# Pooled attention and a GELU MLP: key pools of batches 3 to 7 turned by a transposing DMA, with pools kept at 72 rows per head

## Chip, cores and metric

The kernel runs on one core of a Trainium2 chip. The metric is the device time of one launch in microseconds (us); lower is better. Names used below: PE is TensorE's matmul stream, PEld its weight loads, DVE is VectorE, ACT is ScalarE, POOL is GpSimd, SP is SyncE, which in this kernel only issues DMAs.

## What is computed

Attention over pooled keys and values, then a two-layer MLP with a tanh GELU, in float32 at the borders:

```python
# q, k, v: (8 batches, 8 heads, 576 rows, 64); pool = 8, so Sp = 72 pools per head
k_p = k.reshape(B, H, Sp, 8, D).mean(axis=3);  v_p = v.reshape(B, H, Sp, 8, D).mean(axis=3)
scores = (1 / sqrt(D)) * q @ k_p.T ;  attn = exp(scores - max);  attn /= attn.sum(-1) + 1e-9
x = (attn @ v_p).transpose(0, 2, 1, 3).reshape(4608, 512)
h = x @ w_in                                   # 512 -> 2048
g = 0.5 * h * (1 + tanh(sqrt(2/pi) * (h + 0.044715 * h**3)))
out = g @ w_out                                # 2048 -> 512, 4608 rows
```

## The kernel before, in words

**Stages.** The order of instructions is written out by hand: every engine runs its instructions in the order in which the program issues them, and a DMA instruction that has to wait holds back everything behind it on the engine that issues it. After a prologue (batch 0's attention) there are nine groups, g = 0 to 8, each of 512 rows of x (a batch has 576). A group has two phases on PE. P1 (`p1_mm`, line 332; `gelu`, line 338) is 64 matmuls of 512 columns, x times `w_in`, with one GELU on ACT for each of 16 blocks `fo`. P2 (`p2_mm`, line 343; `store`, line 349) is 64 matmuls of 512 columns, g times `w_out`, in four row tiles r of 16 matmuls, each copied out of PSUM by DVE into a tile `osb` and stored by four DMAs on SP. The attention of the next batch, nb = g + 1, is spread over P2: at the positions `pos = (6, 14, 20, ...)` of line 506, counted in P2 matmuls, `qk` makes the scores of one pair of heads for half a batch, `expo` takes exp on ACT, and one position later `av` multiplies with the pooled v (which also holds columns of 8.0, so that the sums come out beside the products); `norm` and `mult` divide. So the first `qk` of a batch stands before P2 matmul 6, the first `av` before P2 matmul 14. Groups 7 and 8 have no attention. The last row tile of group 8 is done in two column parts of 384 and 128 columns (line 532).

**What feeds the attention of batch b.** Three loads, issued by POOL in `load_next` (line 449) at the start of group b - 2 (for batch 2 after P1 of group 0; batches 0 and 1 are loaded from the prologue):

- q (`load_q`, line 83), cast to bf16 on the way into `qb`; `trans_q_dma` (line 221) turns it into `qT` by a transposing DMA that SP issues once the load has landed. POOL then waits for `qT` at the copy into `gate` (line 453) before it issues the other loads.
- k (`load_k`, line 67) as 512 + 64 rows of pools, whatever head they belong to: 128 partitions x 4 rows, and the remaining 64 rows in a fifth column of `kt`, beside 64 rows of v.
- v (`load_v`, line 78), pools 0 to 63 of each head.

In group b - 1, DVE adds up the eight rows of each pool: `k_steps` (line 140; 1280, 640 and 320 elements per partition) at fo 2 and 3, giving `kp`, and `v_steps` (line 154) at fo 7 and 8, giving the main part of `vp`. The last 8 pools of v, which lie in `kp`, are moved into rows of `vp` by two small DMAs that SP issues (`v_moves`, line 148). PE turns `kp` at fo 9 by five transposes (`trans_k_mm`, line 169), and DVE copies the result into the two weight tiles `kTs` (`trans_k_copy`, line 175, 12 copies a batch, most of them small). Because the v rows of heads 4 to 7 are kept in a rotated order on 128 partitions, `kTs`, `vp` and `ones` have 128 columns or rows for these heads (`pool_rows`, line 231).

**Order on the two queues around the change.** On SP, in each group: the `qT` transposing DMA of batch g + 2, the two `v_moves` of batch g + 1, then the 16 stores of the group. On POOL, in each group: the load of q, the copy into `gate`, the loads of k and v. Batch 1 differs: its q is transposed on PE in group 0 (fo 12 to 15), and its v is loaded by SP from the prologue (line 422), held back by a one-element memset of `vt` on DVE (line 421).

Of the kernel before, what the change touches and what calls it, by code (L numbers as in the profile page):

```python
# [18 lines left out]
def kernel(  # L19
# [23 lines left out]
    KR = 4  # L43
# [9 lines left out]
    opool = ctx.enter_context(tc.tile_pool(name="op", bufs=6))  # L53
# [11 lines left out]
    kts = [consts.tile([128, KR + 1, 512], F32, name=f"kt{i}") for i in range(2)]  # L65

    def load_k(b, engs):
        rows = k[b].rearrange("h (j l) d -> (h j) (l d)", l=8)
        main = rows[0:128 * KR].rearrange("(p r) c -> p r c", r=KR)
        n = KR // len(engs)  # L70
        for i, eng in enumerate(engs):
            eng.dma_start(out=kts[b % 2][:, i * n:(i + 1) * n], in_=main[:, i * n:(i + 1) * n])
        engs[0].dma_start(out=kts[b % 2][64:128, KR], in_=rows[128 * KR:])
        rows = v[b].rearrange("h (j l) d -> j h (l d)", l=8)
        for i in range(2):
            engs[-1].dma_start(out=kts[b % 2][32 * i:32 * i + 32, KR], in_=rows[64:, 4 * i:4 * i + 4])  # L76
# [41 lines left out]
    kTs = [[consts.tile([128, H, 128], BF16, name=f"kT{i}{e}") for e in range(2)] for i in range(2)]  # L118
    kps = [consts.tile([128, KR + 2, D], BF16, name=f"kp{i}") for i in range(2)]

    vps = [consts.tile([128, H, 2, D], BF16, name=f"vp{i}") for i in range(2)]

    vz = consts.tile([128, H, 2, D], BF16, name="vz")
    ones = consts.tile([128, 2, 3, D], BF16, name="ones")
# [6 lines left out]
    for half, j0, j1 in ((0, 0, 128), (1, 0, 8), (1, 64, 128)):  # L131
        nc.vector.memset(ones[j0:j1, half, 1], 8.0)
# [14 lines left out]

    def v_moves(b):

        for i in range(2):  # L150
            nc.sync.dma_start(out=vps[b % 2][64 - 64 * i:72 - 64 * i, 4 * i:4 * i + 4, 0],
                              in_=kps[b % 2][32 * i:32 * i + 32, KR])

    def v_steps(b):
        t = vts[b % 2]
        w = (vps[b % 2] if b else vz)[:, :, 0]

        def main():
            for i in range(2):
                p = slice(64 * i, 64 * i + 64)  # L160
                add(w[p, 4 * i:4 * i + 4], t[p, :, 0:64], t[p, :, 64:128])

        return [lambda: add(t[:, :, 0:256], t[:, :, 0:256], t[:, :, 256:512]),
                lambda: add(t[:, :, 0:128], t[:, :, 0:128], t[:, :, 128:256]), main]
# [10 lines left out]
    def trans_k_copy(b, e, bank, lower=True, upper=True):  # L175


        tp = half_bank(bank)[0:D, 0:(KR + 1) * 128].rearrange("p (r c) -> p r c", c=128)
        o = kTs[b % 2][e][e * 64:(e + 1) * 64]
        copy = nc.vector.tensor_copy  # L180

        def heads(h0, h1, c0, j0, j1):
            copy(out=o[:, h0:h1, c0:c0 + (j1 - j0) * KR].rearrange("p h (j r) -> p h j r", r=KR),  # L183
                 in_=tp[:, 0:KR, h0 * KH:h1 * KH].rearrange("p r (h j) -> p h j r", j=KH)[:, :, j0:j1])

        if lower:
            heads(0, 4, 0, 0, KH)
        if upper:
            heads(4, H - 1, 64, 0, 16)
            heads(4, H - 1, 0, 16, KH)  # L190
            copy(out=o[:, H - 1, 64:72].rearrange("p (j r) -> p j r", r=KR),
                 in_=tp[:, 0:KR, (H - 1) * KH:128].rearrange("p r j -> p j r"))
            copy(out=o[:, H - 1, 72:128], in_=tp[:, KR, 64:120])
            copy(out=o[:, H - 1, 0:8], in_=tp[:, KR, 120:128])
# [36 lines left out]
    def pool_rows(pr):  # L231
        return Sp if pr < PR // 2 else 128

    def qk(b, c, pr, bank):
        for e in range(2):
            h = 2 * pr + e
            n = pool_rows(pr)
            nc.tensor.matmul(out=PS[:n, bank + e, :CH].rearrange("j (t p) -> j t p", p=32),  # L238
                             lhsT=kTs[b % 2][c][:, h, :n],
                             rhs=qTs[b][:, h // 4, :, h % 4 * 32:h % 4 * 32 + 32],  # L240
                             start=True, stop=True)

    def expo(b, c, pr, bank):
        n = pool_rows(pr)
        e = ep.tile([128, 2, CH], BF16, name="e", bufs=8)
        nc.scalar.activation(out=e[:n], in_=PS[:n, bank:bank + 2, :CH], func=ACT.Exp, scale=1.0 / 64.0)  # L246
        es[b, c, pr] = e
# [6 lines left out]
    def av(b, c, pr, bank):  # L254


        e = es.pop((b, c, pr))
        n = pool_rows(pr)
        for x in range(2):
            nc.tensor.matmul(out=PS[:, bank + x, :CH], lhsT=window(vps[b % 2][:n], 2 * pr + x),  # L260
                             rhs=e[:n, x, :], start=True, stop=True)
# [20 lines left out]
    def den0(c, pr, bank):  # L282
        for x in range(2):
            e = es[0, c, pr + x]
            n = pool_rows(pr)
            for y in range(2):
                one = ones[:n, pr // 2].rearrange("j a d -> j (a d)")[:, 64 - 64 * y:192 - 64 * y]
                nc.tensor.matmul(out=PS[:, bank + x, :CH], lhsT=one, rhs=e[:n, y, :],
                                 start=(y == 0), stop=(y == 1))
# [8 lines left out]
    def av0(c, pr, bank):  # L298
        for x in range(2):
            e = es.pop((0, c, pr + x))  # L300
            n = pool_rows(pr)
            for y in range(2):
                nc.tensor.matmul(out=PS[:, bank + x, :CH], lhsT=window(vz[:n], 2 * (pr + x) + y),
                                 rhs=e[:n, y, :], start=(y == 0), stop=(y == 1))
# [27 lines left out]
    def p1_mm(g, fo, ko, c0=0, c1=GROUP):  # L332
        r0 = g * GROUP
        q, j = divmod(fo % 8, 4)
        nc.tensor.matmul(out=PS[:, h_bank(g, fo), c0:c1], lhsT=w_in_b[fo // 8][:, ko, q * 512 + j:(q + 1) * 512:4],  # L335
                         rhs=xT[:, ko, r0 + c0:r0 + c1], start=(ko == 0), stop=(ko == KO - 1))
# [10 lines left out]
    osbs = {}  # L347

    def store(g, r, bank, c0=0, c1=DM):
        if (g, r) not in osbs:  # L350
            osbs[g, r] = opool.tile([128, DM], F32, name="osb")
        osb = osbs[g, r]
        nc.vector.tensor_copy(out=osb[:, c0:c1], in_=PS[:, bank, c0:c1])  # L353

        for n in range(4):
            b, col = divmod(g * GROUP + r * 128 + n * 32, S)
            rows = out[b * S:(b + 1) * S].rearrange("(p t e) d -> e t p d", t=TP, e=2)
            eng = nc.scalar if c1 - c0 < DM and n % 2 else nc.sync
            eng.dma_start(out=rows[col // CH, col % CH // 32, :, c0:c1], in_=osb[n * 32:(n + 1) * 32, c0:c1])
# [30 lines left out]
    for h in range(H):  # L390
        i = h // 4
        nc.tensor.matmul(out=PS[64 - 64 * i:72 - 64 * i, 7, h * D:(h + 1) * D],
                         lhsT=identb[0:64, 32 * i + h % 4:32 * i + 32:4], rhs=kps[0][0:64, KR],
                         start=True, stop=True)
# [3 lines left out]
    for i in range(2):  # L398
        p = slice(64 - 64 * i, 72 - 64 * i)
        nc.vector.tensor_copy(out=vz[p, 4 * i:4 * i + 4, 0],  # L400
                              in_=PS[p, 7, 256 * i:256 * i + 256].rearrange("p (h d) -> p h d", d=D))
# [18 lines left out]

    nc.vector.memset(vts[1][:, 0, 0:1], 0.0)
    load_v(1, [nc.sync])
# [13 lines left out]
    for w in vps:  # L436
        nc.vector.memset(w, 8.0)
        nc.vector.memset(w[0:64, H // 2:], 0.0)
        nc.vector.memset(w[0:8, H // 2:], 8.0)
# [5 lines left out]
    for g in range(NG):  # L445
# [3 lines left out]
        def load_next():  # L449

            load_q(g + 2)
            trans_q_dma(g + 2)
            nc.gpsimd.tensor_copy(out=gate, in_=qTs[g + 2][0:1, 1, TP - 1, 0:2])  # L453
            load_k(g + 2, [nc.gpsimd])
            load_v(g + 2, [nc.gpsimd])

        if 0 < g and g + 2 < B:
            load_next()
# [3 lines left out]
        if nb is not None:  # L462
            kk = k_steps(nb)
# [3 lines left out]
            if g:  # L467
                plan = {2: kk[:1], 3: kk[1:], 7: vv[:1], 8: vv[1:], 9: tk}
            else:
                tq = [lambda a=a, i=i: trans_q(nb, *a, (5, 6, 7, 5)[i], nc.vector) for i, a in enumerate(QG)]  # L470
                plan = {0: kk, 12: tq[:1], 13: tq[1:2] + tk, 14: tq[2:3], 15: tq[3:] + vv}
# [13 lines left out]
        for fo, ko in first:  # L485
            p1_mm(g, fo, ko)
        for fo in range(FO):
            if fo >= 4:
                for ko in range(KO):
                    p1_mm(g, fo, ko)  # L490
# [41 lines left out]
    for c0, c1, bank in ((0, 384, o_bank(g, 3)), (384, DM, 4)):  # L532
        for fo in range(FO):
            p2_mm(g, 3, fo, bank, c0, c1)
        store(g, 3, bank, c0, c1)
# [30 lines left out]
```

The softmax here doesn't subtract the row's maximum and nothing guards it: scores larger than these inputs give would overflow.

## Time and profile before

| | before |
|---|---|
| median of 3 runs | 307.33 us (307.14 to 310.01) |
| the profiled execution: its own time | 307.9 us |
| its span in the profile | 306.1 us |
| PE busy | 296.8 us (97%) |
| PEld busy | 157.6 us (51%) |
| DVE busy | 150.5 us (49%) |
| ACT busy | 219.0 us (72%) |
| POOL busy | 35.0 us (11%) |
| P1 to P2 to next P1, group 3 (first matmuls) | 119.29, 133.39, 151.13 us |
| 128x512 matmuls, lines 335 and 344 | 126.6 and 133.9 us busy |

The span runs from the first to the last instruction of the trace; the execution's own time is 1.8 us longer. "Busy" of PE counts the modelled length of matmuls that overlap, so distances between starts say more than lengths: two consecutive matmuls of 512 columns start 0.216 us apart. A line of the timeline gives the start, the length, the engine, the source line, the operation and its tiles, and how many instructions it sums up; the brackets give the idle time before them and who ended it. A DMA stands in the timeline with the time that its issue took on the issuing engine (SPq, ACTq, POOL), not with its transfer. In lists of groups the columns are line, engine, operation, tiles, shapes, count, busy us, mean ns, and idle time before.

### The profile page before, as it was taken

How to read it: one execution, taken by the hardware profiler on the slowest of the kernel's cores; microseconds unless marked ns; L12 is line 12 of the kernel's file. 1: busy time of each engine (PE TensorE's matmuls, PEld its weight loads, DVE VectorE, ACT ScalarE, POOL GpSimd, SP SyncE). 2: the span in 40 equal slices, each digit the busy share in tenths (PEclk: the TensorE clock that was granted, in tenths of full speed). 3: DMA queues.
4: the chain of work that ended last, by engine and by line, in shares of the span. 5: the costliest groups of instructions: out<-in, count | busy, mean ns of one | idle time of the engine just before them, and what ended most of it. 6: DMA issues, size and time to landing. Idle time of an engine off the chain costs nothing.

```text
span 306.1 us, 4354 instructions
## 1 busy us (share of the span) xinstructions
PE 296.8 (97%) x1528; PEld 157.6 (51%) x1557; DVE 150.5 (49%) x336; ACT 219.0 (72%) x402; POOL 35.0 (11%) x67
## 2 busy tenths in 40 slices
PE   8999899999999999999999999999999999999994
PEld 3555455555555555555555555555555555445543
DVE  5885757572577057805682559245932630120012
ACT  1687489867987798779977898789868986206500
POOL 7102002305003200320014000400000000000000
PEclk9999999999999999999999999999999999999999
DMA  7999987977955962696159827672101210121022
GB/s 221 266 254 264 227 171 139 310 168 184 257 138 113 278 154 53 118 279 154 35 112 250 181 61 103 203 153 71 35 1 36 59 44 0 36 70 35 2 68 69
DMA packets 30806, 41.12 MB, mean 134 GB/s; under 512 B 18176, under 2 KB 18432, under 8 KB 29888
## 3 DMA queue, kind: packets, MB, share of 16 engines
q0 software_dynamic: 7568, 24.38, 33.7%
q1 hardware_dynamic: 22528, 15.14, 21.1%
q10 hardware_dynamic: 688, 1.31, 1.3%
q8 instruction: 12, 0.20, 0.3%
q14 instruction: 10, 0.08, 0.1%
HBM read 36.70 MB, written 9.44 MB: 151 GB/s over the span
## 4 chain that ended last, share of the span: by engine, by line
PE 87%; DMA 11%; issue 1%; ACT 0%; DVE 0%; POOLq 0%
PE PS L344 40%; PE PS L335 37%; DMA qb<-in_q_dram 11%; PE PS L238 5%; PE PS L260 4%; PE PS L173 1%; PE PS L203 0%; ACT e L246 0%; ACT ld L268 0%; ACT ld L267 0%; DVE osb L353 0%; POOLq L550 0%
## 5 line engine op out<-in xcount | busy, mean ns | idle before, releaser
L344 PE MATMUL PS<-w_out_b,gT 128*128 128x512 bf16 (+2 forms) x577 | 133.9, 373 | 0.7
L335 PE MATMUL PS<-xT,w_in_b 128*128 128x512 bf16 x563 | 126.6, 379 | 0.7
L341 ACT ACTIVATE gT<-PS 128x512 bf16<-128x512 f32 x144 | 81.2, 603 | 48.1 <-PE PS L335 48.0
L335 PEld LDWEIGHTS <-w_in_b 128*128 128x128 bf16 x576 | 64.7, 113 | 57.2
L344 PEld LDWEIGHTS <-gT 128*128 128x128 bf16 x592 | 57.0, 97 | 55.7 <-issue 0.4
L353 DVE COPY osb<-PS 128x512 f32<-128x512 f32 (+2 forms) x37 | 25.1, 677 | 98.2 <-PE PS L344 78.6
L278 DVE TENSOR_TENSOR xT<-PS,rc 64x288 bf16<-64x288 f32 x112 | 50.9, 455 | 31.7 <-ACT rc L270 27.5
L246 ACT ACTIVATE e<-PS 72x576 bf16<-72x576 f32 (+1 forms) x64 | 41.0, 647 | 8.8 <-PE PS L238 7.9
L238 PE MATMUL PS<-qT,kT 128*72 128x288 bf16 (+1 forms) x128 | 25.8, 286 | 0.9 <-ACT qT L213 0.6
L270 ACT ACTIVATE rc<-ld 128x288 f32<-128x288 f32 x56 | 24.8, 444 | 1.8
L313 ACT ACT_TABLE_LOAD x17 | 21.8, 1283 | 4.3 <-issue 4.1
L267 ACT ACTIVATE ld<-PS 64x288 f32<-64x288 f32 x56 | 22.8, 408 | 1.3
L268 ACT ACTIVATE ld<-PS 64x288 f32<-64x288 f32 x56 | 22.5, 402 | 1.4
L260 PE MATMUL PS<-e,vp 72*128 72x288 bf16 (+1 forms) x112 | 23.1, 286 | 0.0
L138 DVE TENSOR_TENSOR kt<-kt 128x1280 f32<-128x1280 f32 (+5 forms) x18 | 18.9, 1048 | 7.6 <-DMA kt<-in_v_dram 4.6
L238 PEld LDWEIGHTS <-kT 128*72 128x72 bf16 (+1 forms) x128 | 13.2, 105 | 15.1 <-DVE qT L215 1.2
L453 POOL COPY gate<-qT 1x2 bf16<-1x2 bf16 x6 | 1.0, 174 | 138.5 <-DMA qT<-qb 138.5
L138 DVE TENSOR_TENSOR vt<-vt 128x1024 f32<-128x1024 f32 (+1 forms) x16 | 15.3, 956 | 1.7 <-DMA vt<-in_v_dram 1.4
L183 DVE COPY kT<-PS 64x288 bf16<-64x288 bf16 (+2 forms) x48 | 13.0, 318 | 6.2 <-PE PS L173 6.0
L260 PEld LDWEIGHTS <-vp 72*128 72x128 bf16 (+1 forms) x112 | 11.0, 98 | 3.8
L365 PE MATMUL PS<-idle 128*128 128x512 bf16 x32 | 10.4, 468 | 1.6 <-DVE idle L126 1.2
L76 POOL DMA_DIRECT2D kt<-in_v_dram x14 | 8.0, 586 | 0.1
(48 smaller groups left out, 88.8 us busy)
## 6 DMA issues: line engine op xcount, KB each, us to landing
out_dram<-osb SPq DMA_DIRECT2D x140, 64.0 KB
kt<-in_k_dram POOLq DMA_DIRECT2D x7, 1024.0 KB, 6.0
vt<-in_v_dram POOLq DMA_DIRECT2D x12, 512.0 KB, 8.7
qb<-in_q_dram POOLq DMA_DIRECT2D x7, 576.0 KB, 11.8
w_in_b<-in_moe_w_in_dram POOLq DMA_DIRECT2D x2, 1024.0 KB, 16.8
w_out_b<-in_moe_w_out_dram POOLq DMA_DIRECT2D x4, 512.0 KB, 19.3
vt<-in_v_dram SPq DMA_DIRECT2D x3, 512.0 KB
kt<-in_k_dram POOLq DMA_DIRECT2D x7, 128.0 KB, 6.0
```

The costliest lines, as they stand in the source:

```text
L138: nc.vector.tensor_tensor(out=o, in0=a, in1=b, op=ALU.add)
L238: nc.tensor.matmul(out=PS[:n, bank + e, :CH].rearrange("j (t p) -> j t p", p=32), lhsT=kTs[b % 2][c][:, h, :n], rhs=qTs[b][:, h // 4, :, h ...
L246: nc.scalar.activation(out=e[:n], in_=PS[:n, bank:bank + 2, :CH], func=ACT.Exp, scale=1.0 / 64.0)
L260: nc.tensor.matmul(out=PS[:, bank + x, :CH], lhsT=window(vps[b % 2][:n], 2 * pr + x), rhs=e[:n, x, :], start=True, stop=True)
L267: nc.scalar.activation(out=ld[0:64], in_=PS[64:128, bank, :CH], func=ACT.Ln)
L268: nc.scalar.activation(out=ld[64:128], in_=PS[0:64, bank + 1, :CH], func=ACT.Ln)
L270: nc.scalar.activation(out=rc, in_=ld, func=ACT.Exp, scale=-1.0)
L278: nc.vector.tensor_tensor(out=xT[rows, pr, col:col + CH], in0=PS[rows, bank + x, :CH], in1=rc[rows], op=ALU.mult)
L335: nc.tensor.matmul(out=PS[:, h_bank(g, fo), c0:c1], lhsT=w_in_b[fo // 8][:, ko, q * 512 + j:(q + 1) * 512:4], rhs=xT[:, ko, r0 + c0:r0 + c ...
L341: nc.scalar.activation(out=gTs[g][:, fo, :], in_=PS[:, h_bank(g, fo), :], func=ACT.Gelu_apprx_tanh)
L344: nc.tensor.matmul(out=PS[:, bank, c0:c1], lhsT=gTs[g][:, fo, r * 128:(r + 1) * 128], rhs=w_out_b[:, fo, c0:c1], start=(fo == 0), stop=(fo ...
L353: nc.vector.tensor_copy(out=osb[:, c0:c1], in_=PS[:, bank, c0:c1])
```

## The change

Four things change.

1. **Keys of batches 3 to 7** (`KX = 3`). k is loaded with 72 pools of each head on 72 partitions, 8 heads side by side (`load_k_dma`). DVE adds it there (2048, 1024 and 512 elements per partition), writes the pools into a zeroed tile `kz` and copies them to a second place in it (`k_steps_dma`, now at fo 0); SP issues a transposing DMA from `kz` into `kx`, whose blocks are the weights of `qk`. PE's five transposes and DVE's copies of these batches go. The last 8 pools of v go to partitions 96 to 127 of `kt`, are added by three more small instructions, and moved into `vp` by two DMAs as before.
2. **Order.** For nb of 3 and later, `load_next` is issued after the transposing DMA of `kz`, not at the start of the group, and begins with a copy into `gate` that reads `kx`. On SP the order of such a group is: `kx` of batch g + 1, `qT` of batch g + 2, the two `v_moves` of batch g + 1, the 16 stores. In group 6 there is no load any more.
3. **v and the pool rows.** v keeps its 72 rows in order; `kTs`, `vp`, `vz` and `ones` shrink to 72 rows or columns; the k copies of batches 0 to 2 are 8 a batch, `v_moves` of batches 1 and 2 one DMA. v of batch 1 is loaded (by SP) after the first add of batch 1's k in group 0. `osb` has 5 buffers instead of 6. POOL zeroes `kz` once.
4. **The last group.** P1 of group 8 is done in 384 + 128 columns for every fo, the last 128 read from `xT` with a step of 32 elements, so that the last row tile's rows come out in another order; its P2 is done in 256 + 256 columns, each half stored by one DMA (the first by ACT, the second by SP) instead of four.

```diff
+    kts = [consts.tile([128, H, 512], F32, name=f"kt{i}") for i in range(2)]
+    KX = 3
...
-        for i in range(2):
-            engs[-1].dma_start(out=kts[b % 2][32 * i:32 * i + 32, KR], in_=rows[64:, 4 * i:4 * i + 4])
+        engs[-1].dma_start(out=kts[b % 2][0:64, KR], in_=rows[64:])
+
+    def load_k_dma(b):
+        nc.gpsimd.dma_start(out=kts[b % 2][0:Sp], in_=k[b].rearrange("h (j l) d -> j h (l d)", l=8))
+        rows = v[b].rearrange("h (j l) d -> j h (l d)", l=8)
+        for y in range(2):
+            nc.gpsimd.dma_start(out=kts[b % 2][96:128, y], in_=rows[64 + 4 * y:68 + 4 * y])
...
+    def k_steps_dma(b):
+        t = kts[b % 2]
+        k0, k1 = (kz[0:Sp, :, e, e * D:e * D + D] for e in range(2))
+        m, x = t[0:Sp], t[96:128, 0:2]
+        return [lambda: add(m[:, :, 0:256], m[:, :, 0:256], m[:, :, 256:512]),
+                lambda: add(m[:, :, 0:128], m[:, :, 0:128], m[:, :, 128:256]),
+                lambda: add(k0, m[:, :, 0:64], m[:, :, 64:128]),
+                lambda: nc.vector.tensor_copy(out=k1, in_=k0),
+                lambda: trans_k_dma(b),
+                lambda: add(x[:, :, 0:256], x[:, :, 0:256], x[:, :, 256:512]),
+                lambda: add(x[:, :, 0:128], x[:, :, 0:128], x[:, :, 128:256]),
+                lambda: add(kps[b % 2][96:128, 0:2], x[:, :, 0:64], x[:, :, 64:128])]
...
+    def trans_k_dma(b):
+        kxs[b] = bp.tile([128, 2 * H, 128], BF16, name="kx")
+        nc.sync.dma_start_transpose(out=kxs[b], in_=kz.rearrange("p h e c -> p (h e c)"))
+
     def v_moves(b):
-        for i in range(2):
-            nc.sync.dma_start(out=vps[b % 2][64 - 64 * i:72 - 64 * i, 4 * i:4 * i + 4, 0],
-                              in_=kps[b % 2][32 * i:32 * i + 32, KR])
+        if b >= KX:
+            for y in range(2):
+                nc.sync.dma_start(out=vps[b % 2][64 + 4 * y:68 + 4 * y, :, 0], in_=kps[b % 2][96:128, y])
+            return
+        nc.sync.dma_start(out=vps[b % 2][64:Sp, :, 0], in_=kps[b % 2][0:64, KR])
...
-                             lhsT=kTs[b % 2][c][:, h, :n],
+                             lhsT=kxs[b][:, 2 * h + c, 0:Sp] if b >= KX else kTs[b % 2][c][:, h],
...
+        if turned:
+            out, x = out.rearrange("f (p t) -> f p t", p=32), x.rearrange("k (t p) -> k p t", p=32)
...
         def load_next():
+            if nb >= KX:
+                nc.gpsimd.tensor_copy(out=gate, in_=kxs[nb][0:1, 2 * H - 1, 0:2])
             load_q(g + 2)
             trans_q_dma(g + 2)
             nc.gpsimd.tensor_copy(out=gate, in_=qTs[g + 2][0:1, 1, TP - 1, 0:2])
-            load_k(g + 2, [nc.gpsimd])
+            if g + 2 >= KX:
+                load_k_dma(g + 2)
+            else:
+                load_k(g + 2, [nc.gpsimd])
             load_v(g + 2, [nc.gpsimd])
-        if 0 < g and g + 2 < B:
+        if 0 < g and nb is not None and nb < KX:
             load_next()
...
-            kk = k_steps(nb)
+            kk = k_steps(nb) if nb < KX else k_steps_dma(nb)
             kk.append(lambda: v_moves(nb))
-            if g:
+            if nb >= KX:
+                plan = {0: kk[:5] + ([load_next] if g + 2 < B else []), 1: kk[5:], 7: vv[:1], 8: vv[1:]}
+            elif g:
                 plan = {2: kk[:1], 3: kk[1:], 7: vv[:1], 8: vv[1:], 9: tk}
             else:
+                kk.insert(1, lambda: (nc.vector.memset(vts[1][:, 0, 0:1], 0.0), load_v(1, [nc.sync])))
...
+            if g + 1 == NG:
+                for c0, c1, turned in ((0, 384, False), (384, GROUP, True)):
+                    for ko in range(KO):
+                        p1_mm(g, fo, ko, c0, c1, turned)
...
-    for c0, c1, bank in ((0, 384, o_bank(g, 3)), (384, DM, 4)):
+    for c0, bank in ((0, o_bank(g, 3)), (256, 4)):
+        c1 = c0 + 256
         for fo in range(FO):
             p2_mm(g, 3, fo, bank, c0, c1)
-        store(g, 3, bank, c0, c1)
+        osb = opool.tile([128, 256], F32, name="osb")
+        nc.vector.tensor_copy(out=osb, in_=PS[:, bank, c0:c1])
+        b, col = divmod(N - 128, S)
+        t = col % CH // 32
+        rows = out[b * S:(b + 1) * S].rearrange("(p t e) d -> e p t d", t=TP, e=2)
+        (nc.sync if c0 else nc.scalar).dma_start(out=rows[col // CH, :, t:t + 4, c0:c1], in_=osb)
```

## Prediction

> **What bounds the kernel now.** I read the page first (shares and chain), then the timelines of SP, POOL, DVE and PE in one group, then DVE's groups by form, because the change moves work between exactly these queues.
>
> The page:
>
> ```profile
> span 306.1 us, 4354 instructions
> ...
> PE 296.8 (97%) x1528; PEld 157.6 (51%) x1557; DVE 150.5 (49%) x336; ACT 219.0 (72%) x402; POOL 35.0 (11%) x67
> ...
> PEclk9999999999999999999999999999999999999999
> ...
> PE 87%; DMA 11%; issue 1%; ACT 0%; DVE 0%; POOLq 0%
> ```
>
> PE is the bound from 34 us to the end, at full clock; the 11% of DMA lie in the first 34 us. So removed work pays only if PE did it, and a wait costs only if it stands in front of a PE instruction. The next three views show such a wait nearly happening. The timeline of SP alone, 60 to 76 us (group 1):
>
> ```profile
> 67.11 2.66 SPq L223 DMA_TRANSPOSE qT<-qb  x1
> 69.87 1.41 SPq L151 DMA_DIRECT2D vp<-kp  x2
> 74.82 1.25 SPq L359 DMA_DIRECT2D out_dram<-osb  x3
> ```
>
> The timeline of DVE alone, and that of PE alone, over the same group:
>
> ```profile
> 62.35 0.49 DVE L138 TENSOR_TENSOR kp<-kt 128x320 bf16<-128x320 f32 x1
> ```
>
> ```profile
> 55.61 8.80 PE L335 MATMUL PS<-xT,w_in_b 128*128 128x512 bf16 x39
> ...
> 69.71 1.46 PE L344 MATMUL PS<-w_out_b,gT 128*128 128x512 bf16 x6
> ...
> 73.22 0.41 PE L260 MATMUL PS<-e,vp 72*128 72x288 bf16 x2
> ```
>
> `kp` was complete at 62.84, yet its two moves to `vp` were issued only at 69.87, 7 us later, right behind the `qT` transpose, which SP held until q had landed (SP's own waits for this group: 7.5 us for q). The first `av`, which reads the moved rows, came at 73.22, 17.61 us after P1 began at 55.61. In this one group the moves still made it, by about 1 us. In groups 2 to 6 q had landed long before, and SP issued `qT` and the moves early.
>
> POOL's timeline gives the latency of the transpose: issued at 67.11, its result lets the gate copy go at 71.77, and the next DMA issue follows at 72.25:
>
> ```profile
> 71.77 0.17 POOL L453 COPY gate<-qT 1x2 bf16<-1x2 bf16 x1 [15.70 <-DMA qT<-qb]
> 72.25 0.57 POOL L72 DMA_DIRECT2D kt<-in_k_dram  x1 [0.30 <-issue]
> ```
>
> DVE's groups by form give the price per element of the adds:
>
> ```profile
> L138 DVE TENSOR_TENSOR kt<-kt 128x1280 f32<-128x1280 f32 x7 | 10.4, 1492 | 4.8 <-DMA kt<-in_v_dram 4.6
> L138 DVE TENSOR_TENSOR vt<-vt 128x1024 f32<-128x1024 f32 x8 | 9.8, 1220 | 1.4 <-DMA vt<-in_v_dram 1.4
> L183 DVE COPY kT<-PS 64x288 bf16<-64x288 bf16 x16 | 7.2, 449 | 5.9 <-PE PS L173 5.7
> ...
> L138 DVE TENSOR_TENSOR kt<-kt 128x640 f32<-128x640 f32 x7 | 5.8, 826 | 0.2
> L138 DVE TENSOR_TENSOR vt<-vt 128x512 f32<-128x512 f32 x8 | 5.5, 693 | 0.3
> ...
> L215 DVE COPY qT<-PS 128x512 bf16<-128x512 bf16 x4 | 1.7, 420 | 0.8 <-PE PS L203 0.8
> ```
>
> **The change part by part.** *The new chain in groups 2 to 5* (batches 3 to 6; they still load a batch). The q load now stands behind the landing of `kx`, `qT` behind that load, and `v_moves` behind `qT` on SP. I count from the start of P1, with group 3's rows (P1 at 119.29).
>
> - DVE ends the last `mult` of the batch before at 121.70: +2.4.
> - Three adds of 2048, 1024 and 512 elements. 1492 ns for 1280 and 826 for 640 make 1.04 ns an element plus 0.16 us: 2.29 + 1.23 + 0.69 = 4.2. The copy of 512 bf16 elements has no row from SBUF; 0.2 to 0.6, I take 0.3 (the copy from PSUM took 0.42). `kz` is done at +6.9.
> - SP is free (its last store of the group before was issued by 122.5). `kx` has 16 blocks where `qT` has 18: 4.66 us from issue to gate, scaled 4.1; I take 4.3 of 4.1 to 4.7. +11.2. `qk` needs it at +15.1 (134.68 - 119.29 less 0.28), so that wait stays hidden.
> - From gate to next POOL issue 0.48: +11.7.
> - The q load by itself: from issue to first packet 1.3 us (k load issued at 97.11, first packets after 98.4), 0.59 MB at the 0.205 MB a us that the DMA view shows for q and v between 103 and 110 us makes 2.9, and some 0.6 to the signal: 4.9. Bounds 4.4 and 7.3, the shortest of the trace's q loads, which had company. +16.6.
> - `qT`'s issue 2.76 (67.11 to 69.87), two moves 1.41, landing 0.9 (0.5 to 1.2; the queue's last packet after these moves fell just past 72.0): +21.7.
> - `av` wants the rows at 136.90 - 119.29 = 17.6, less the transposes that go: +17.3.
>
> PE therefore stands 4.4 us at the first `av` of each batch, with all P2 matmuls behind it: 4 x 4.4 = **+17.6**, bounds 3.2 and 7.8 each (12.8 to 31.2). Group 6 loads nothing, so its moves follow `kx` directly, and groups 0 and 1 keep their order. Also queued behind `qT` on SP are the 16 stores; the first is due at +18.5, after the held `av`, so they cost nothing of their own. On POOL the k and v loads move to +21.8; k's 72 partitions may take 2.3 us longer than its 6.0 (v, on 64 partitions with the same 2 KB pieces, moved at 0.2 MB a us, k at 0.4), which gives +30, and DVE needs it at 36 + 2.4. Hidden by 8 us.
>
> *The clock over these stalls.* The longest idle of PE in this trace, 1.4 us before 33.73, left it at full clock; its first 12 matmuls after the start were 0.427 apart instead of 0.216, 2.3 us lost. A stall of 4.4 lies between: 0 to 2.3 each, I take 0.6, nearer the row that kept it: **+2.4** (0 to 9.2). The Trainium skill (TensorE: Matmul & The Clock Gate, What's actually happening) says that an idle window of about 3.4 us puts the array at half speed; a stall as long as mine could trip it each time, and the sum would then be some 7 us higher. No row here shows a stall of that length.
>
> *PE's transposes.* Five of them cost 0.28 us a batch (127.93 to 128.21 in P1): 5 x 0.28 = **-1.4**, the only PE work that goes.
>
> *DVE, POOL.* The k work of such a batch rises from 2.8 to about 5.9 us, its 2.6 us of `kTs` copies go. DVE sat idle 7.28 us before its first P2 copy (130.4 to 137.8): 0; without that cover, 0.5 a batch. The memset of `kz` falls into POOL's 21.3 us wait for `qT` of batch 2, but stands ahead of q's load: 0, since the queue ran full until 44 us.
>
> *The head.* PE waited 1.41 us for batch 1's q at 33.7; without v's 1 MB in the same queue k and q of batch 1 come sooner, and some 0.2 of DVE copies go: -1.6. But v of batch 1, before issued at 19.03 and moved from 22 to 32 us, is now issued near 27. At the same pace it lands near 40, and 2.4 us of adds put the first `av` of group 0 at 42.8 against 39.6: +3.2. Sum +1.6 at worst assumption, -1.6 if v lands by 37; I take **+1.0** (-1.6 to +2.0).
>
> *The last group.* In the trace 384 columns took 0.1625 and 128 took 0.0558 a matmul (the tail's 16 + 16): 64 x 0.0023 = +0.15. The turned 128 columns are read at a step of 32 elements. PE's weight loads with a step of 4 took 113 ns against 97 for plain ones; the same 16% is +0.6. DVE's strided 288-element copy ran at half the rate per element of the plain one; that would be +3.6. I take 0.6, the row on the same engine: **+0.75** (0.15 to 3.75). The Trainium skill (SBUF - State Buffer, Door 1: The DMA port swizzle) says that SBUF is read in 16-byte lines and that leaving a line at each access is penalised; a step of 64 bytes does that, so by the page the 3.6 end is the likelier and the sum 3.0 higher. In the tail the last copy is 0.13 longer, and one issue follows it instead of two a queue (303.55 to about 303.05): **-0.3** (-0.6 to 0).
>
> Sum against the profiled 307.9: 307.9 + 17.6 + 2.4 - 1.4 + 1.0 + 0.75 - 0.3 = 327.95. The median of the runs is 0.6 lower than that execution: **327.4 us**.
>
> **The rivals.**
>
> - *Not slower: the moves are not held.* If vp's rows are there by +17.3, the stall and the clock term go: 327.4 - 20.0 = 307.4, no change, and a little faster if the head is at its good end. It decides at 4.4 us less chain, which the q load alone (4.9) would nearly have to give. Against it stands group 1, where SP held ready moves for 7 us.
> - *Stall under half as long.* q by itself at 4.4, `kx` at 3.5, k's adds starting earlier: 2 us a stall, no clock loss: 327.4 - 9.6 - 2.4 = 315.4.
> - *`kx` late as well.* If the transpose of `kz` takes 8.5 instead of 4.3, it meets `qk` at +15.1 and pushes the chain on: 4 x 4.2 = 16.8 more, 344. Against: six transposes of `qT` had issue times within 2.66 to 2.87.
> - *Clock lost at each stall and the turned columns at half rate*: + 6.8 + 3.0 = 337.
>
> **How the numbers follow.** The forecast, stalls of 3.2 to 7.8 with the clock open: 0.80, its own range 317 to 342 (the 337 case is inside). Short stalls 0.08, `kx` late 0.05, not held 0.07. The range 316 to 343 leaves out the unheld case and the far tail. A run of this kernel can tell 1% from no change; the unheld case splits into faster 0.03 and same 0.04, slower 0.93 is all the rest.
>
> **What would show it.** SP: `qT` issued some 10 us after `kx`, `vp<-kp` right behind it. POOL: gate on `kx` near +11, then the q load. PE: a gap of 4 us before the first `av` (72x288) of groups 2 to 5 and none in group 6; matmuls 0.427 apart after it if the clock falls. No L173 after group 1. I am wrong if q lands within 1 us of its issue, or if PE's gap stands elsewhere: at `qk`, in group 0, or in P1 of group 8.

## The result, and the profile after

The changed kernel takes 358.06 us (median of 4 runs, 356.87 to 358.62) against 307.29 us before: ratio 1.162, 95% interval 1.156 to 1.168. It is slower, as forecast, but by 50.8 us and not by 20. The profiled execution took 356.87 us with a span of 355.1 us, 49.0 longer than the span before.

The page of the changed kernel, with the lines that answer to those shown of before:

```profile
span 355.1 us, 4412 instructions
...
PE 318.9 (90%) x1596; PEld 168.5 (47%) x1596; DVE 152.6 (43%) x277; ACT 220.1 (62%) x402; POOL 35.8 (10%) x65
...
PEclk9999969999999699987999899978999999999999
...
PE 66%; DMA 21%; DVE 5%; SPq 4%; POOL 1%; issue 1%; DVEq 0%; POOLq 0%
```

PE's share fell to 90%, and PE's clock, full throughout before, dips five times. Two causes stand side by side on this page: PE waits, and then it works at half speed. A fall of the busy share alone would not show the second, because slow matmuls count as busy. For the same reason the page hides a third, slow matmuls at full clock in group 8; the table has it.

Where the 49.0 us are, from the starts of P1 and P2 in the two traces (the rows are rounded one by one):

| stretch | before | changed | difference | forecast |
|---|---|---|---|---|
| to P1 of group 0 | 20.94 | 21.23 | +0.3 | in the head |
| group 0 | 34.68 | 42.52 | +7.8 | +1.0 (head) |
| group 1 | 31.84 | 31.85 | 0 | 0 |
| groups 2 to 5, each | 31.84 | 39.30, 40.03, 38.78, 39.97 | +30.7 in all | +18.9 (17.6 + 2.4 - 1.1) |
| group 6 | 31.84 | 31.58 | -0.3 | -0.3 |
| group 7 | 27.63 | 27.63 | 0 | 0 |
| group 8, P1 | 13.81 | 24.41 | +10.6 | +0.75 |
| group 8, P2 and tail | 18.0 | 17.8 | -0.2 | -0.3 |

**The forecast wait, in group 2.** Before the change SP issued `qT` and the moves of this group early, as its timeline shows (P1 began at 87.45):

```profile
91.89 2.71 SPq L223 DMA_TRANSPOSE qT<-qb  x1
94.70 1.39 SPq L151 DMA_DIRECT2D vp<-kp  x2
```

The timelines of SP, POOL and DVE in the changed kernel, where P1 of this group begins at 95.60, each a view of its own:

```profile
102.74 1.83 SPq L173 DMA_TRANSPOSE kx<-kz  x1
113.23 2.72 SPq L246 DMA_TRANSPOSE qT<-qb  x1
116.05 1.38 SPq L179 DMA_DIRECT2D vp<-kp  x2
```

```profile
107.14 0.18 POOL L456 COPY gate<-kx 1x2 bf16<-1x2 bf16 x1 [27.57 <-DMA kx<-kz]
107.59 0.73 POOL L93 DMA_DIRECT2D qb<-in_q_dram  x1 [0.28 <-issue]
117.93 0.18 POOL L459 COPY gate<-qT 1x2 bf16<-1x2 bf16 x1 [9.61 <-DMA qT<-qb]
```

```profile
98.02 3.54 DVE L146 TENSOR_TENSOR kt<-kt 72x2048 f32<-72x2048 f32 x2
101.67 0.69 DVE L146 TENSOR_TENSOR kz<-kt 72x512 bf16<-72x512 f32 x1
102.39 0.29 DVE L163 COPY kz<-kz 72x512 bf16<-72x512 bf16 x1
...
103.89 0.29 DVE L146 TENSOR_TENSOR kp<-kt 32x128 bf16<-32x128 f32 x1
```

Read them as one chain: DVE ends `kz` at 102.7, SP issues `kx`, POOL sees it at 107.14 and issues q at 107.59, q lands at 113.2, SP issues `qT` and only then the two moves. Their source was ready at 104.2, 12 us earlier. PE at the same time:

```profile
112.68 0.41 PE L257 MATMUL PS<-qT,kx 128*72 128x288 bf16 x2
118.80 0.64 PE L277 MATMUL PS<-e,vp 72*128 72x288 bf16 x2 [5.71 <-DMA vp<-kp]
119.23 2.77 PE L362 MATMUL PS<-w_out_b,gT 128*128 128x512 bf16 x6
```

`av` wanted to start at about 112.9, 17.3 us after P1. The last line is the second loss: six matmuls in 2.77 us, where six took 1.46 before. The table by stretches (columns: the stretch and its length; busy time and count of PE, PEld, DVE, ACT and POOL; PE's granted clock; DMA share; GB/s) puts a number on it:

```profile
113.10:118.80 5.70, 0.01 (x1) 0.04 (x2) 0.00 (x0) 0.65 (x1) 0.45 (x2) 0.74 0.55 105
118.80:122.60 3.80, 3.80 (x12) 1.78 (x13) 1.60 (x3) 1.34 (x4) 3.10 (x5) 0.50 0.50 130
122.60:134.00 11.40, 11.40 (x63) 6.15 (x62) 5.93 (x12) 10.71 (x23) 0.00 (x0) 1.00 0.97 209
```

The clock falls while PE waits and stays at 0.50 for 3.8 us of work. The list of waits of the changed kernel has the same wait four times, and one that I had thought small:

```profile
DVE vt L146 <- DMA vt<-in_v_dram: 8.1, 1, 8.1
...
PE PS L277 <- DMA vp<-kp: 22.4, 4, 5.7
...
PE PS L277 <- DVE vp L146: 7.6, 1, 7.6
```

The last line is group 0. Before the change SP issued v of batch 1 at 19.03 and DVE added it at 38.56 without a wait; here SP issued it at 29.79, DVE could add it up from 45.16 only, and PE stood at the first `av` from 40 to 47.6. SP's and DVE's timelines of the changed kernel:

```profile
29.79 1.26 SPq L88 DMA_DIRECT2D vt<-in_v_dram  x2
```

```profile
45.16 1.95 DVE L146 TENSOR_TENSOR vt<-vt 128x1024 f32<-128x1024 f32 x2 [8.05 <-DMA vt<-in_v_dram]
```

### The profile page after: what moved, and what is told of

Its sections match the earlier page's. It is cut to its first block, busy times and chain, and to the rows that moved or that the text cites. A ratio compares the mean times of both kernels' runs of the same rounds, so it can differ in the third digit from the quotient of the medians.

```text
span 355.1 us, 4412 instructions
## 1 busy us (share of the span) xinstructions
PE 318.9 (90%) x1596; PEld 168.5 (47%) x1596; DVE 152.6 (43%) x277; ACT 220.1 (62%) x402; POOL 35.8 (10%) x65
## 4 chain that ended last, share of the span: by engine, by line
PE 66%; DMA 21%; DVE 5%; SPq 4%; POOL 1%; issue 1%; DVEq 0%; POOLq 0%
PE PS L362 32%; PE PS L354 26%; DMA kt<-in_v_dram 6%; PE PS L277 4%; DMA vt<-in_v_dram 4%; PE PS L257 3%; DMA qb<-in_q_dram 3%; SPq L246 3%; DMA out_dram<-osb 3%; DMA kx<-kz 2%; DVE kt L146 2%; DMA vp<-kp 2%; DVE osb L367 1%; SPq L179 1%; DVE xT L295 1%
## 5 line engine op out<-in xcount | busy, mean ns | idle before, releaser
L362 PE MATMUL PS<-w_out_b,gT 128*128 128x512 bf16 (+1 forms) x592 | 144.2, 389 | 0.0
L354 PE MATMUL PS<-xT,w_in_b 128*128 128x512 bf16 (+2 forms) x640 | 137.0, 375 | 0.0
L367 DVE COPY osb<-PS 128x512 f32<-128x512 f32 x35 | 24.2, 692 | 136.8 <-PE PS L362 131.0
L295 DVE TENSOR_TENSOR xT<-PS,rc 64x288 bf16<-64x288 f32 x112 | 51.0, 455 | 34.9 <-ACT rc L287 32.5
L264 ACT ACTIVATE e<-PS 72x576 bf16<-72x576 f32 x64 | 41.0, 646 | 20.6 <-PE PS L257 19.6
L277 PE MATMUL PS<-e,vp 72*128 72x288 bf16 x112 | 25.0, 306 | 30.1 <-DMA vp<-kp 22.4
L284 ACT ACTIVATE ld<-PS 64x288 f32<-64x288 f32 x56 | 22.8, 408 | 30.1 <-PE PS L277 28.8
L146 DVE TENSOR_TENSOR kt<-kt 72x2048 f32<-72x2048 f32 (+9 forms) x28 | 30.4, 1084 | 7.4 <-DMA kt<-in_k_dram 3.4
L277 PEld LDWEIGHTS <-vp 72*128 72x128 bf16 x112 | 11.1, 102 | 35.0 <-issue 23.5
L257 PE MATMUL PS<-qT,kx 128*72 128x288 bf16 x80 | 17.3, 300 | 0.0
L257 PEld LDWEIGHTS <-kx 128*72 128x72 bf16 x80 | 9.6, 120 | 10.0 <-issue 2.1
L257 PE MATMUL PS<-qT,kT 128*72 128x288 bf16 x48 | 9.7, 290 | 0.9 <-ACT qT L236 0.6
## 6 DMA issues: line engine op xcount, KB each, us to landing
kt<-in_k_dram POOLq DMA_DIRECT2D x5, 1152.0 KB, 11.9
```

The lines of the kernel that those rows point to most:

```text
L146: nc.vector.tensor_tensor(out=o, in0=a, in1=b, op=ALU.add)
L257: nc.tensor.matmul(out=PS[:Sp, bank + e, :CH].rearrange("j (t p) -> j t p", p=32), lhsT=kxs[b][:, 2 * h + c, 0:Sp] if b >= KX else kTs[b % ...
L264: nc.scalar.activation(out=e, in_=PS[:Sp, bank:bank + 2, :CH], func=ACT.Exp, scale=1.0 / 64.0)
L284: nc.scalar.activation(out=ld[0:64], in_=PS[64:128, bank, :CH], func=ACT.Ln)
L295: nc.vector.tensor_tensor(out=xT[rows, pr, col:col + CH], in0=PS[rows, bank + x, :CH], in1=rc[rows], op=ALU.mult)
L354: nc.tensor.matmul(out=out, lhsT=w, rhs=x, start=(ko == 0), stop=(ko == KO - 1))
```

## The experiments

"The changed kernel" is the reference of each edit; times are medians, ratios are to the kernel before.

**The moves first.** In groups 2 to 5 the moves are issued ahead of the q transpose:

```diff
-                plan = {0: kk[:5] + ([load_next] if g + 2 < B else []), 1: kk[5:], 7: vv[:1], 8: vv[1:]}
+                plan = {0: kk[:5], 1: kk[5:] + ([load_next] if g + 2 < B else []), 7: vv[:1], 8: vv[1:]}
```

> One edit to the changed kernel: in groups 2 to 5 the two moves of v's last rows are issued by SP before the transposing DMA of the next batch's q, not behind it. Theory (SP's order): the 5.7 us that PE stands at the first av of these groups are the moves held behind a DMA that waits for q; they and the half-speed clock after them go, 4 x 7.5 to 8: about 358 - 31 = 327 us, no gap over 1 us at av in groups 2 to 5, no half-speed stretch there, and the gap in group 0 stays. Rival (DMA traffic): the rows are late because the small packets of the transposing DMAs fill the queue that the moves share; then the order of issue gives back at most the 1.4 us of the moves' own landing per group: 350 us or more.

Measured: 329.77 us, ratio 1.072 (1.070 to 1.073). With the moves ahead of a `qT` that waits for q, no wait at `av` is left in these groups: their place on SP is the cause. But only groups 2 and 3 reach 31.58 us; group 4 takes 32.21 and group 5 takes 35.58. Three timelines of this kernel, POOL, DVE and PE, show what is late next:

```profile
186.59 0.89 POOL L80 DMA_DIRECT2D kt<-in_k_dram  x1 [0.43 <-issue]
```

```profile
198.41 3.54 DVE L146 TENSOR_TENSOR kt<-kt 72x2048 f32<-72x2048 f32 x2 [5.24 <-DMA kt<-in_k_dram]
```

```profile
208.23 0.69 PE L257 MATMUL PS<-qT,kx 128*72 128x288 bf16 x2 [2.18 <-DMA kx<-kz]
```

k was issued at 186.59 and added from 198.41, 11.8 us later; PE then waits at `qk`. Adds of k, `kx`, q, `qT`, load of k form a loop from one batch to the next: in this trace its links run from the adds at 198.41 to the q issue at 208.76, the k issue at 219.82 and the next adds at 230.90. That is 32.5 us; the three turns before, with adds at 97.84, 131.39 and 165.32, took 33.6, 33.9 and 33.1. All are more than the 31.6 of a group, so each batch comes later in its group than the one before, until PE waits for it. The stalls of the changed kernel, with groups of 39 to 40 us, had covered it.

**The wait filled with work.** Dummy matmuls before the first `av` of batches 3 to 6:

```diff
+                    if i == 1 and KX <= nb < B - 1:
+                        at(pos[i], spin, 25, 4)
                     at(pos[i], av, *a)
```

> One edit to the changed kernel: 25 dummy matmuls of 512 columns (5.4 us at full clock) stand before the first av of batches 3 to 6, so that PE waits with work instead of idle. The wait itself stays. Theory (the clock falls when PE stands idle that long): half-speed stretches in groups 2 to 5 go, which cost about 1.7 to 2 us each: about 358 - 7 = 351 us, and the stretch in group 0 stays. Rival (the waits alone are the loss, the clock record costs nothing): 358 us, within 1.

Measured: 347.64 us, ratio 1.130 (1.128 to 1.133). PE's timeline in group 2 of this kernel:

```profile
112.16 5.56 PE L378 MATMUL PS<-idle 128*128 128x512 bf16 x25
117.86 0.41 PE L277 MATMUL PS<-e,vp 72*128 72x288 bf16 x2
118.10 1.46 PE L362 MATMUL PS<-w_out_b,gT 128*128 128x512 bf16 x6
```

The wait ends where it did, and the six matmuls behind it take 1.46 us again. Groups 2 to 5 fall from 39.5 on average to 37.3, so the clock alone had cost 2.2 each, 8.9 in all; the rest of the 10.4 us lies in group 0 (42.0 for 42.5) and between executions. Half the length of the half-speed work after the four waits of the changed kernel (3.8, 5.7, 3.2 and 5.2 us by its granted clock) adds up to the same 8.9.

**No stepped read.** The 128-column part of P1 in group 8 reads x in its stored order:

```diff
-                for c0, c1, turned in ((0, 384, False), (384, GROUP, True)):
+                for c0, c1, turned in ((0, 384, False), (384, GROUP, False)):
```

> One edit to the changed kernel: the 128-column part of P1 in group 8 reads x in its stored order instead of with a step of 32 elements; number and size of matmuls and weight loads stay. The last 128 rows of the output come out in another order. Theory (the step): the 64 stepped matmuls, 0.217 us apart, go to 0.056: about 358 - 10.3 = 347.7 us. Rival (splitting a matmul into 384 and 128 columns, with 64 more weight loads, is the cost): 358 us.

Measured: 346.43 us, ratio 1.127 (1.123 to 1.132). The same 64 matmuls in PE's groups by form, first in the changed kernel, then in this one:

```profile
L354 PE MATMUL PS<-xT,w_in_b 128*128 128x128 bf16 x64 | 16.6, 392 | 0.0
```

```profile
L354 PE MATMUL PS<-xT,w_in_b 128*128 128x128 bf16 x64 | 6.2, 219 | 0.0
```

P1 of group 8 falls from 24.41 to 13.97 us: the split costs 0.16, the stepped read 10.4. The remaining 1.2 us of the difference lie elsewhere and are of the size by which executions of the changed kernel differ (356.87 to 358.62).

**v of batch 1 early.** Its load goes back to the prologue:

```diff
     mult0(0, 0, 4)
+    nc.vector.memset(vts[1][:, 0, 0:1], 0.0)
+    load_v(1, [nc.sync])
...
-                kk.insert(1, lambda: (nc.vector.memset(vts[1][:, 0, 0:1], 0.0), load_v(1, [nc.sync])))
```

> One edit to the changed kernel: v of batch 1 is loaded from the prologue again, as before the change. Theory (issued too late): the 7.6 us at the first av of group 0 and about 1.7 us of half clock after it go, and the 1.4 us wait for batch 1's q comes back: about 358 - 8 = 350 us. Rival (the queue's backlog: the same bytes are late wherever v stands, because the weights fill the queue): the wait only moves to q or to w_out, gain under 3 us: 355 us or more.

Measured: 348.66 us, ratio 1.133 (1.129 to 1.136). Group 0 takes 33.31 us instead of 42.52. SP issued v at 19.40, and DVE adds it without a wait, as its timeline in this kernel shows:

```profile
37.29 1.94 DVE L146 TENSOR_TENSOR vt<-vt 128x1024 f32<-128x1024 f32 x2
```

In this execution the wait for batch 1's q, 1.4 us before the change, did not come back. The time of issue, not the backlog, was the cause.

**No wait for kx.** The copy that holds back the q load goes, the order on SP stays:

```diff
-            if nb >= KX:
-                nc.gpsimd.tensor_copy(out=gate, in_=kxs[nb][0:1, 2 * H - 1, 0:2])
```

> One edit to the changed kernel: POOL's copy that waits for kx before the q load is gone; the order on SP stays (kx, qT of the next batch, the moves of v). Theory (the order on SP costs only because the q load starts behind kx): q has landed long before, qT is issued right behind kx and the moves some 13 us after P1 begins, before av needs them at 17.4; groups 2 to 5 take 31.6 us each, 358 - 32 = 326 us, and k's loads, issued some 6 us earlier in a group than with the gate, aren't late in groups 4 and 5, as they are when only the moves are put first (329.8 us). Rival (qT in front of the moves is enough to make them late, by its issue and its packets): gaps of 1 us or more at av stay, over 332 us.

Measured: 325.24 us, ratio 1.058 (1.055 to 1.060). Groups 2 to 6 all take 31.57 or 31.58 us. SP's timeline of this kernel in group 2, and PE's:

```profile
103.08 1.79 SPq L173 DMA_TRANSPOSE kx<-kz  x1
105.04 3.32 SPq L246 DMA_TRANSPOSE qT<-qb  x1
108.46 1.39 SPq L179 DMA_DIRECT2D vp<-kp  x2
```

```profile
113.01 0.41 PE L257 MATMUL PS<-qT,kx 128*72 128x288 bf16 x2
113.26 0.41 PE L277 MATMUL PS<-e,vp 72*128 72x288 bf16 x2
```

The moves still stand behind `qT`, but `qT` no longer waits. So here a place behind a transpose is harmless; a place behind a transpose that waits for a load is not. This edit also takes q out of the loop that made k late, which moving the moves did not: POOL issues k of group 2 at 110.86, 14.9 us after P1, where with the moves first it was 22.8 us (118.19 after P1 at 95.42).

**All k on TensorE.** Changes 3 and 4 alone, with the keys and the order of the loads as before:

```diff
-    KX = 3
+    KX = 8
...
-        if 0 < g and nb is not None and nb < KX:
+        if 0 < g and g + 2 < B:
```

> The changed kernel with k of all batches turned by TensorE and the loads of the next batch issued at the start of a group: the other three changes alone. Theory (the stalls belong to the transposing DMA and the order that came with it): groups 1 to 6 take 31.85 us as before, the losses in group 0 (some 9 us with the clock) and in P1 of group 8 (10.5) stay: 307.5 + 19 = 326 to 327 us. Rival (the 72-row pools or the smaller set of output buffers cost something in every group): groups longer than 31.9 us, over 329 us.

Measured: 326.48 us, ratio 1.061 (1.058 to 1.063). Groups 1 to 6 take 31.85 or 31.86 us, as before the change: 72 pools a head and five output buffers neither cost nor give anything there. The 31.6 us to the changed kernel belong to changes 1 and 2, the transposing DMA and the order that came with it.

**The step, measured.** Other columns of x, two blocks of four matmuls for each step:

```diff
...
+                step = (1, 2, 4, 8, 16, 32, 0, 0)[fo // 2]
...
+                                     rhs=xT[:, ko, 0:128 * step:step], start=(ko == 0), stop=(ko == KO - 1))
```

> The changed kernel with the 128-column part of P1 in group 8 reading x at steps of 1, 2, 4, 8, 16 and 32 elements (two blocks of four matmuls each), and as in the change for the last four blocks; the columns read are others, so the last 128 rows of the output are not the reference's. Theory (lines): 0.056 us a matmul while two or more elements lie in 16 bytes (steps 1 to 4), then slower, 0.11 to 0.22 from a step of 8 on, the same for 8, 16 and 32. Rival (the inner run of only 4 elements and the jump after it, not the step, costs): steps to 32 all near 0.056, and only the change's own pattern 0.217.

One execution, 355.01 us. PE's timeline of this kernel; each L511 line is four stepped matmuls, and the distance to the next line's start is what they took:

```profile
314.86 0.39 PE L511 MATMUL PS<-xT,w_in_b 128*128 128x128 bf16 x4
315.08 0.81 PE L354 MATMUL PS<-xT,w_in_b 128*128 128x384 bf16 x4
...
316.61 0.40 PE L511 MATMUL PS<-xT,w_in_b 128*128 128x128 bf16 x4
316.84 0.81 PE L354 MATMUL PS<-xT,w_in_b 128*128 128x384 bf16 x4
...
318.38 0.64 PE L511 MATMUL PS<-xT,w_in_b 128*128 128x128 bf16 x4
318.84 0.83 PE L354 MATMUL PS<-xT,w_in_b 128*128 128x384 bf16 x4
...
320.63 1.08 PE L511 MATMUL PS<-xT,w_in_b 128*128 128x128 bf16 x4
321.53 0.83 PE L354 MATMUL PS<-xT,w_in_b 128*128 128x384 bf16 x4
...
326.94 1.03 PE L511 MATMUL PS<-xT,w_in_b 128*128 128x128 bf16 x4
327.79 0.83 PE L354 MATMUL PS<-xT,w_in_b 128*128 128x384 bf16 x4
```

Steps 1, 2, 4, 8 and 32 in this order: 0.22, 0.23, 0.46, 0.90 and 0.85 us for four matmuls, or 0.055, 0.058, 0.115, 0.225 and 0.21 each. Step 16 gave 0.23, the change's own pattern 0.22 each. The step is the cost, not the short inner run: a plain step of 32 is as slow as the change's own pattern. My expectation that step 4 is free was wrong, since it already doubles the time.

**The three losses undone.** No wait for `kx`, v of batch 1 early, P1 and tail of group 8 as before:

```diff
...
+    nc.vector.memset(vts[1][:, 0, 0:1], 0.0)
+    load_v(1, [nc.sync])
...
-                nc.gpsimd.tensor_copy(out=gate, in_=kxs[nb][0:1, 2 * H - 1, 0:2])
...
-                kk.insert(1, lambda: (nc.vector.memset(vts[1][:, 0, 0:1], 0.0), load_v(1, [nc.sync])))
...
-                for c0, c1, turned in ((0, 384, False), (384, GROUP, True)):
...
+    for c0, c1, bank in ((0, 384, o_bank(g, 3)), (384, DM, 4)):
...
```

> The changed kernel with its three losses undone: no wait for kx before the q load, v of batch 1 loaded from the prologue, P1 and the last row tile of group 8 as before. Left of the change: k of batches 3 to 7 through the transposing DMA, and 72 pools per head. Theory: the five sets of transposes that PE no longer does (0.28 us each, 1.4) are all that is left, less 0.3 for a later prologue: 306.2 us against 307.4, faster by 0.4%. Rival (contention: the added packets on the queue of SP cost PE or DVE as much as the transposes did): 307.4 or more.

Measured: 307.57 us beside 307.61 of before, ratio 0.9988 (0.9972 to 1.0005): no difference that can be told, so neither the theory's 0.4% nor the rival is shown. Its profiled execution has groups 2 to 6 at 31.57 or 31.58 us, so the 0.27 a group is there, 1.3 us in all. That execution was the fastest of its 12 times, which run from 306.25 to 308.27; the others have no profile. One thing that differs between executions is the wait for batch 1's q in group 0: 1.4 us before the change, two of 0.3 here, 1.5 in the profile of the next kernel. It is as large as the gain; whether it is what takes the gain back isn't shown.

**Turned by ACT.** The version above, with the tail of 256 + 256 columns and one store each, the rows turned where ACT writes the GELU:

```diff
...
+        h = PS[:, h_bank(g, fo), :]
+        if g + 1 == NG:
+            nc.scalar.activation(out=gTs[g][:, fo, 0:384], in_=h[:, 0:384], func=ACT.Gelu_apprx_tanh)
+            nc.scalar.activation(out=gTs[g][:, fo, 384:512].rearrange("f (p t) -> f t p", p=32),
+                                 in_=h[:, 384:512].rearrange("f (t p) -> f t p", p=32), func=ACT.Gelu_apprx_tanh)
...
```

> The version with the three losses undone (307.57 us beside 307.61 before), and the last row tile of group 8 in 256 + 256 columns, each half stored by one DMA, as in the change; but the order of its 128 rows is turned where ACT writes the GELU (two activations for each of 16 blocks, the second one writing with a step of 4 elements) and not where PE reads x. Theory: PE reads x and g without a step, P1 of group 8 takes 13.8 us, ACT's two activations (some 0.49 + 0.27, by lines 128x512 0.60 and 128x288 0.41) fit into the 0.86 us of a block, and the 0.28 us that the tail gained in the changed kernel stay: 307.3 us, too little to tell from 307.6. Rival (ACT's write with a step, or its second activation, is slow): ACT needs over 0.86 us a block, P1 or the first P2 matmuls of group 8 wait, 309 us or more.

Measured: 306.50 us beside 307.68 of before, ratio 0.9962 (0.9948 to 0.9977): the fastest of the kernels here, though the gain on before is only 1.2 us or 0.4%. ACT's timeline shows two activations of a block in 0.65 us, under the 0.86 that PE takes:

```profile
278.18 0.60 ACT L361 ACTIVATE gT<-PS 128x384 bf16<-128x384 f32 x1
278.66 0.47 ACT L362 ACTIVATE gT<-PS 128x128 bf16<-128x128 f32 x1
278.83 0.61 ACT L361 ACTIVATE gT<-PS 128x384 bf16<-128x384 f32 x1
```

P1 of group 8 takes 13.81 us. The tail explains some 0.3 of the 1.1 us to the version without it; the rest isn't explained. In this execution the first `av` of group 1 waited 0.4 us for its moves, the near miss that the prediction had read in the kernel before.

## Why the prediction was right in direction and wrong in size

- **The stall in groups 2 to 5: right place, mechanism and number of stalls, short by 1.4 us each.** Counted from P1 as in the prediction (group 2, P1 at 95.60): DVE free +2.4 (forecast +2.4), `kz` +7.1 (+6.9), gate on `kx` +11.5 (+11.2), q issued +12.0 (+11.7), q landed +17.6 (+16.6), `av` +23.2 (+21.7), wanted at +17.3 (+17.3). The terms mis-sized are "the q load by itself ... 4.9", which took 5.6 (its own parts, 1.3, 2.9 and 0.6, add up to 4.8, and no row was given for the last), and the landing of the moves, "0.9", which took 1.4 after their issue: in the record of DMA packets those of `qT` (256 bytes) run until about 117.4 and those of the moves (128 bytes), on the same queue, until about 118.5. Counted from the +17.3, four waits of 5.6 to 5.9 us make 23.1 where 17.6 was the forecast. The edit of SP's order and the removed wait confirm the cause from two sides.
- **The clock: the step failed.** "I take 0.6, nearer the row that kept it: +2.4." Each of the four stalls lost the clock; refilling them gave back 2.2 each, 8.9 in all. I had a row on either side of 4.4 us and leaned to the wrong one; the stated upper bound, 9.2, holds. The Trainium skill (TensorE: Matmul & The Clock Gate, What's actually happening) was right against my choice: all five stalls here, of 5.5 to 7.6 us, were followed by half speed. Its window of about 3.4 us isn't the shortest wait that does it, though: one of 2.2 us did too (last section).
- **The head: the step failed.** "At the same pace it lands near 40." SP issued v at 29.79, not near 27, because it stands behind the first add of batch 1's k, and the data of `kt` for that add were there only at 28.25. DVE could start on v at 45.16, 15.4 us after the issue, where "27" to "40" counts 13; in the trace of before, too, 14 us had passed from the issue at 19.03 to v's last bytes at about 33. The stall was 7.6 us instead of 3.2, and the half clock came on top: +7.8 for group 0 where I took +1.0 for all of the head, outside my bound of +2.0.
- **The last group: the step failed.** "I take 0.6, the row on the same engine." The stepped matmuls cost 10.4 us more, four times the plain ones. My upper bound, half rate, came from DVE's copies, and the row that I chose was of weight loads with a step of 4; neither says what a matmul pays for its moving operand (the one that streams through, here x) at a step of 32. The bound of 3.75 was too low by a factor of nearly three. The page of the skill (SBUF - State Buffer, Door 1: The DMA port swizzle) had the direction right, but two hits in a 16-byte line weren't enough to keep the speed: bf16 at a step of 4 took twice as long.
- **Right:** the transposes that go (0.27 a group in group 6 and in the versions with the losses undone; 0.28 forecast), the tail (-0.2 for -0.3), no cost of DVE's longer adds, `qk` not waiting for `kx`, stores and k loads covered in the changed kernel. The k load was covered although it was mis-sized: it took 11.9 us, where the forecast allowed 8.3, and the margin of 8 us absorbed it.
- The sum of the misses: 23.1 - 17.6 = 5.5 for the stalls, 8.7 - 2.4 = 6.3 for the clock (what of the +30.7 is neither stall nor transposes), 7.8 + 0.3 - 1.0 = 7.1 for the head, 10.6 - 0.75 = 9.8 for P1 of group 8. That makes 28.7 of the 29 us between forecast and span. No single one of them explains the miss; the head and P1 of group 8, each outside its own bound, are more than half of it. The prediction had named a gap in either place as a sign that it was wrong.

## What to carry to other kernels

When an instruction is moved in a queue that issues in order, follow what it now waits for, and price everything queued behind it by when its reader needs it: here 1.4 us of small moves held PE for 23 us. Price a stall of PE of a few us with the half-speed work after it (here 2.2 us for each of 5.7), and read a matmul's moving operand in its stored order, turning data where another engine writes it anyway. After a stall is taken away, add up the loop from one batch to the next once more: the next limit (here 32.5 to 33.9 us of loads and transposes against 31.6 of PE) had been hidden by it.

## What the runs showed of the hardware

- The step of a bf16 moving operand: a matmul of 128 columns took 0.055 us at step 1, 0.058 at 2, 0.115 at 4, 0.21 to 0.23 at 8, 16 and 32.
- Every wait of PE of 5.2 us and longer in these traces was followed by half speed. In each trace the granted clock changes only at points that lie a multiple of 3.41 us apart, so a half-speed stretch after one of the four waits of the changed kernel lasted two such intervals (6.8 us) or one (3.4), and of nearly equal waits one cost 1 us more than another (groups of 40.03 and 38.78 us). Waits for batch 1's q of 1.4 us, in the kernel before, and of 1.5 us, in the last one, did not touch the clock. A wait of 2.2 us was enough once, that at `qk` in group 5 of the kernel with the moves first; its table by stretches, from the end of the wait on:

```profile
208.20:211.70 3.50, 3.47 (x10) 1.46 (x11) 0.00 (x0) 0.65 (x1) 0.90 (x2) 0.52 0.43 50
211.70:215.00 3.30, 3.25 (x19) 1.86 (x19) 1.34 (x3) 2.59 (x6) 0.00 (x0) 1.00 0.67 127
```

  The granted clock is 0.52 in the first and 1.00 in the second. What counts seems to be PE's idle time within one interval: the one before this fall (204.75 to 208.16) held 2.1 us of it, while the intervals with the first 1.9 us of a wait, in group 4 of the changed kernel (190.88 to 194.29) and in group 0 of the kernel with all k on TensorE (38.45 to 41.86), were followed by another at full clock. One fall doesn't fit: in the prologue of the kernel without the wait for `kx` it followed an interval with 1.6 us idle and small matmuls (7.35 to 10.76), so the exact rule stays open.
- k on 72 partitions in pieces of 2 KB took 11.9 us from issue to landing (median), before the change 6.0 on 128 partitions; I had allowed 2.3 more. In the kernel with all k on TensorE, on 128 partitions, it is 6.0 again; in the kernels with the new layout it is 11.6 to 12.0, whichever way the loads are ordered. That points to the layout; the number of partitions and the size of the pieces aren't separated by any run.
- ACT wrote bf16 with a step of 4 elements, two activations a block, in 0.65 us a block without holding PE.
